# Transformer layer with linear attention on one core: loads cut in pieces on one queue, Wq transposed mid-stage, one numerator tile at a time, a tabulated unit order

## The chip, the cores and the metric

The kernel runs on one core of one Trainium2 chip. The metric is device time in microseconds (us) of one execution, inputs and outputs in HBM. A core has TensorE (PE, matmuls; its weight loads are PEld), VectorE (DVE), ScalarE (ACT), GpSimd (POOL) and SyncE (SP), which here only issues DMAs. Each engine runs its own instruction list strictly in order; semaphores tie the lists together.

## The reference

One pre-norm layer on x of 2048 rows by 640, all in bf16, with 32 heads of 20 columns:

```
n = layernorm(x);  q, k, v = n @ wqkv             # 640 -> 3 x 640
phi(a) = [softmax(a @ w_phi), softmax(-(a @ w_phi))]   # per head, 20 -> 40 features
o = phi(q) (phi(k)^T v) / (phi(q) . sum_s phi(k) + 1e-6)
h = x + o @ wo
h2 = h + ((layernorm(h) @ w_gate) * (layernorm(h) @ w_up)) @ w_down   # 640 -> 1536 -> 640
```

## The kernel before, in words

The 2048 rows are 16 tiles t of 128; the 640 columns are 5 chunks of 128. Everything is a graph of named units, built in `build_graph`; each unit is a few instructions of one engine. The names that matter:

- **WT, WTe, F1, Fe1** (lines 228 to 261): Wk arrives by rows, PE transposes it (WT), ACT or DVE copies it out (WTe), PE multiplies it with a block-diagonal w_phi (the fold F1), and the copy Fe1 gives the weight that yields k @ w_phi in one step. **wqt, F0, Fe0**: the same for Wq, whose transposes come from six DMA transposes straight from HBM (line 181). All five F0 need all six wqt.
- **x** loads (line 158); **L1s, L1a, L1l, L1e** layernorm statistics on DVE and ACT; **xn** (line 301, DVE) scales a tile to bf16; **xt** transposes it: on PE for the tiles in `TPE` (line 309, copy-out xte on ACT), for the others by a DMA transpose from SP (line 317).
- **K, V** (line 326): projections of a tile, ten matmuls of 320 columns each; **Kx** two exponentials (ACT), **Ks** sums (DVE, line 352), **Kr** reciprocals (DVE), **Kn** the multiply (GpSimd, line 357), **Ve** the copy-out of V (line 343), and **KV** (PE, line 366) accumulates phi(k)^T v over all tiles in three PSUM banks. This is the K/V stage.
- **Q** (line 385): a chunk of q features for 512 rows, then two exponentials Qx (ACT).
- **N** (line 414): numerator and denominator of a tile, two units (s = 1, 0), each with two PSUM banks; DVE combines them by **sr, rho, A, B, dd, rd**; **o** (line 446, GpSimd) divides; **oT** (SP, line 451) transposes; **O** (line 457) is the output projection; **h, L2s, L2a, L2v, L2r, hc, hT** residual, second statistics, centring and a DMA transpose (line 481).
- **U** (line 496): gate and up products in five row blocks (256, 512, 512, 512, 256), **g** copy-out, **u** product (DVE), **D** (line 514) the down projection, **y** (line 526) the scaled residual, **w** the store.

Who runs first is set by `schedule`: an event loop with assumed costs. Each unit has a key; whenever an engine of the loop is free, the ready unit with the lowest key that also finds its buffer slots (`NSLOTS`: PSUM has 8 banks) is appended to that engine's list. The lists are then emitted, with waits, and are what the chip executes in order. A DMA without inputs is ready at once, so its key only places it among other ready DMAs of that queue; SP issues it as soon as it comes up. In the version before, ACT's queue holds the loads of w_phi, of tiles 4 to 15 and of Wo; SP's holds the others.

PE's list before, up to the fourth tile: WT0 WT1 F1_0 F1_1 xt0 WT2 WT3 F1_2 F1_3 WT4 F1_4 F0_0 F0_1 K0 V0 F0_2 F0_3 F0_4 xt1 K1 V1 KV0 K4 V4 K2 V2 KV1 K3 V3 Q0_0. SP's list: x0 wk0 wk2 wk4 wv x1 x2 wqt0 to wqt5 wg wu, then xt4 xt5 xt2 and the other row transposes. All of Q0 stands ahead of KV15 in PE's list.

Of the kernel before, what the change touches and what calls it, by code (L numbers as in the profile page):

```python
# [124 lines left out]
def build_graph():  # L125
# [10 lines left out]


# [101 lines left out]
    FOLD = [(g, 20 * 6 * g, min(20 * 6 * g + 120, 640)) for g in range(6)]
    def fold(kind, i, key, eng):  # L240
# [16 lines left out]
        def fe(e):  # L257
            o = T["Wp"][:, kind, i, :].rearrange("p (b n) -> p b n", b=2)
            if eng == "dve":
                return e.tensor_copy(out=o, in_=pp(b, 0, 320))  # L260
            return e.activation(out=o, in_=pp(b, 0, 320), func=AF.Copy)
        G.op(eng, "Fe%d_%d" % (kind, i), fe, dve_c(640, True) if eng == "dve" else act_c(640), LD, [b], [wp_b[kind][i]], key)
# [35 lines left out]
    for t in range(NT):  # L298
# [5 lines left out]
        if t in TPE:  # L304
            b = Buf("pxt%d" % t, "psum")
            def xt(e, t=t, b=b, xb=xb):
# [6 lines left out]
            G.op("act", "xte%d" % t, lambda e, t=t, b=b: e.activation(  # L313
                out=T["xnT"][:, :, P * t:P * (t + 1)], in_=pb(b).bitcast(BF16)[:, 0:D].rearrange("p (c n) -> p c n", c=NC),
                func=AF.Copy), act_c(640), LA, [b], [xT_b[t]], 10 * t - 20)
# [87 lines left out]
    for t in range(NT):  # L403
        kk = 200 + 12 * t
        q = [i for i, (o0, n) in enumerate(QB) if o0 <= P * t < o0 + n][0]
        nb = {}
# [457 lines left out]
```

## Time and profile before

| what | value |
|---|---|
| median of 3 runs | 313.77 us (310.62 to 314.88) |
| the profiled execution | 312.41 us, span 310.5 us, mean granted clock 0.978 |
| PE busy | 277.5 us, 89% of the span |
| PE weight loads | 182.9 us, 59% |
| DVE busy | 177.6 us, 57% |
| ACT, POOL busy | 107.5 us (35%), 66.6 us (21%) |
| moved by DMA | 22.48 MB |

The page of the profile gives, in this order: busy time by engine; the span in 40 slices with the busy tenths of each engine, the granted clock of PE (in tenths of 2.4 GHz) and DMA activity; the DMA queues; the chain of work that ended last, followed backwards; the costliest groups of instructions with what they waited for; the DMA issues with their time to landing. A line such as L326 is a line of the kernel. SPq stands for SP's instruction queue (its DMA issues), which the page does not count as busy.

### The profile page before, as it was taken

The numbers are of one execution on the slowest core, as the hardware profiler recorded it, in microseconds if no ns is written. First come the engines' busy times: TensorE is split into PE (matmuls) and PEld (weight loads), VectorE is DVE, ScalarE is ACT, GpSimd is POOL, SyncE is SP. The second block draws the span as 40 slices with busy tenths as digits, with TensorE's granted clock in tenths as the row PEclk, the third lists the DMA queues.
The fourth block names the chain that finished last, engine by engine and source line by source line (L and its number), as shares of the span: only waits on it lengthen the run. The fifth ranks groups of instructions, "written<-read, shape, count | busy, mean of one in ns | idle before, by whom it ended". The sixth has DMA issues, their size and how long they took to land.

```text
span 310.5 us, 4962 instructions
## 1 busy us (share of the span) xinstructions
PE 277.5 (89%) x2041; PEld 182.9 (59%) x2058; DVE 177.6 (57%) x357; ACT 107.5 (35%) x189; POOL 66.6 (21%) x71
## 2 busy tenths in 40 slices
PE   3418699999999869979999999799999999999996
PEld 3315567767755538845565477545456754467874
DVE  3743999956547697393645367758454743332332
ACT  3407376555668434345412200223230113210220
POOL 6000267576741323012010011030101100000000
PEclk9857999999999999999999999999999999999999
DMA  8999534500000626122571103242111121001101
GB/s 247 343 222 405 142 65 86 86 1 2 2 0 0 67 52 77 22 44 42 169 149 42 21 5 85 64 62 41 25 21 43 47 61 23 0 0 48 39 2 43
DMA packets 45166, 22.48 MB, mean 72 GB/s; under 512 B 36183, under 2 KB 43863, under 8 KB 45143
## 3 DMA queue, kind: packets, MB, share of 16 engines
q1 hardware_dynamic: 42160, 19.34, 27.3%
q10 hardware_dynamic: 2983, 2.81, 2.9%
q8 instruction: 16, 0.26, 0.4%
q14 instruction: 7, 0.06, 0.1%
HBM read 11.01 MB, written 2.62 MB: 44 GB/s over the span
## 4 chain that ended last, share of the span: by engine, by line
PE 77%; DVE 8%; SPq 6%; DMA 4%; ACT 1%; issue 1%; POOL 1%; DVEq 0%
PE ps L496 33%; PE ps L514 17%; PE ps L326 12%; PE ps L457 6%; PE ps L385 5%; SPq L181 5%; PE ps L366 3%; DVE xn L301 2%; PE ps L414 2%; DVE x_all L461 2%; DMA scratch<-scratch 1%; DMA xnT<-xn 1%; SPq L158 1%; DMA scratch<-in_A_wqkv_dram 1%; DVE st L468 1%
## 5 line engine op out<-in xcount | busy, mean ns | idle before, releaser
L496 PE MATMUL ps<-xnT,Wgu 128*128 128x512 bf16 (+1 forms) x589 | 104.8, 336 | 2.8 <-DVE rs L473 1.9
L496 PEld LDWEIGHTS ps<-xnT,Wgu 128*128 128x128 bf16 x600 | 58.4, 98 | 46.7 <-DVE ev L504 3.4
L504 DVE TENSOR_TENSOR ev<-ps,scratch 128x512 bf16<-128x512 f32 (+1 forms) x60 | 35.0, 584 | 49.4 <-PE ps L496 48.4
L501 ACT ACTIVATE scratch<-ps 128x512 bf16<-128x512 f32 (+1 forms) x60 | 30.7, 511 | 90.7 <-PE ps L496 90.7
L514 PE MATMUL ps<-Wp,ev 128*128 128x320 bf16 x384 | 53.5, 299 | 0.5 <-DVE ev L504 0.5
L326 PE MATMUL ps<-Wp,xnT 128*128 128x320 bf16 x320 | 48.3, 307 | 2.8 <-DMA xnT<-xn 1.8
L357 POOL TENSOR_TENSOR ev<-ev,SR 128x1280 bf16<-128x1280 bf16 x16 | 37.8, 2364 | 44.6 <-DVE SR L355 35.9
L514 PEld LDWEIGHTS ps<-Wp,ev 128*128 128x128 bf16 x384 | 37.3, 98 | 15.5 <-DVE ev L504 0.8
L326 PEld LDWEIGHTS ps<-Wp,xnT 128*128 128x128 bf16 x320 | 31.3, 100 | 15.6 <-DMA xnT<-xn 2.0
L352 DVE TENSOR_REDUCE SR<-ev 128x64 f32<-128x1280 bf16 x16 | 23.7, 1484 | 19.8 <-ACT ev L349 19.7
L446 POOL TENSOR_TENSOR scratch<-scratch,sm 128x640 bf16<-128x640 f32 x16 | 20.2, 1270 | 65.7 <-DVE sm L443 61.6
L526 DVE SCALAR_TENSOR_TENSOR Wp<-ps,rs,x_all 128x640 bf16<-128x640 f32 (+1 forms) x17 | 14.4, 845 | 31.5 <-PE ps L514 31.5
L476 ACT ACTIVATE xn<-x_all,mv 128x640 bf16<-128x640 bf16 x16 | 13.2, 827 | 50.8 <-DVE mv L470 50.8
L349 ACT ACTIVATE ev<-ps 128x640 bf16<-128x640 f32 x32 | 20.8, 700 | 15.2 <-PE ps L326 15.2
L385 PE MATMUL ps<-xnT,Wp 128*128 128x512 bf16 x94 | 22.6, 379 | 3.9 <-DVE sm L429 2.0
L457 PE MATMUL ps<-Wo,scratch 128*128 128x320 bf16 x160 | 23.9, 299 | 1.5 <-DMA scratch<-scratch 0.9
L394 ACT ACTIVATE eqT<-ps 128x512 bf16<-128x512 f32 x40 | 21.6, 594 | 8.8 <-PE ps L385 8.8
L457 PEld LDWEIGHTS ps<-Wo,scratch 128*128 128x128 bf16 x160 | 15.4, 98 | 8.7 <-DMA scratch<-scratch 1.4
L471 POOL TENSOR_SCALAR ln<-mv 128x1 f32<-128x1 f32 x16 | 3.3, 208 | 77.4 <-DVE mv L470 77.4
L461 DVE TENSOR_TENSOR x_all<-ps,x_all 128x640 bf16<-128x640 f32 x16 | 13.1, 818 | 11.2 <-PE ps L457 11.2
L385 PEld LDWEIGHTS ps<-xnT,Wp 128*128 128x128 bf16 x100 | 9.4, 98 | 13.0 <-DVE scratch L432 3.7
L251 PE MATMUL ps<-Phi,scratch 120*128 120x120 bf16 (+3 forms) x70 | 5.0, 238 | 11.6 <-DMA scratch<-in_A_wqkv_dram 9.9
(49 smaller groups left out, 202.1 us busy)
## 6 DMA issues: line engine op xcount, KB each, us to landing
out_dram<-Wp SPq DMA_DIRECT2D x15, 160.0 KB, 1.8
Wgu<-in_B_w_gate_dram SPq DMA_DIRECT2D x1, 1920.0 KB, 9.2
Wgu<-in_B_w_up_dram SPq DMA_DIRECT2D x1, 1920.0 KB, 13.3
Wp<-in_B_w_down_dram SPq DMA_DIRECT2D x1, 1920.0 KB, 8.1
x_all<-in_A_x_dram ACTq DMA_DIRECT2D x1, 1280.0 KB, 13.2
Wp<-in_A_wqkv_dram SPq DMA_DIRECT2D x1, 800.0 KB, 10.1
Wo<-in_A_wo_dram ACTq DMA_DIRECT2D x1, 800.0 KB, 15.6
scratch<-in_A_wqkv_dram SPq DMA_DIRECT2D x2, 320.0 KB, 4.1
```

What stands on the lines that cost most here:

```text
L326: ins = e.matmul(pb(b, hb)[:, 0:320], lhsT=T["xnT"][:, c, P * t:P * (t + 1)], rhs=T["Wp"][:, kind, c, 320 * hb:320 * (hb + 1)], start=(c = ...
L349: G.op("act", "Kx%d_%d" % (t, s), lambda e, s=s, b=b, ek=ek: e.activation(out=T["ek"][:, ek.slots[0], s, :].rearrange("p (b n) -> p b n", ...
L352: G.op("dve", "Ks%d" % t, lambda e, ek=ek, sr=sr: e.tensor_reduce(out=T["SR"][:, sr.slots[0], 0, :], in_=T["ek"][:, ek.slots[0], :, :].rea ...
L357: G.op("pool", "Kn%d" % t, lambda e, ek=ek, sr=sr: e.tensor_tensor(out=T["ek"][:, ek.slots[0], :, :].rearrange("p s (h f) -> p (s h) f", f ...
L385: ins = e.matmul(pb(b)[:, 0:n], lhsT=T["Wp"][:, 0, i, P * c:P * (c + 1)], rhs=T["xnT"][:, i, o0:o0 + n], start=(i == 0), stop=(i == NC - 1))
L394: G.op("act", "Qx%d_%d_%d" % (q, c, s), lambda e, s=s, c=c, o0=o0, n=n, b=b: e.activation(out=T["eqT"][:, s, c, o0:o0 + n], in_=pb(b)[:, 0 ...
L446: G.op("pool", "o%d" % t, lambda e, sm=sm, B=B, o=o: e.tensor_tensor(out=T["o"][:, o.slots[0], :].rearrange("p (h d) -> p h d", d=DH), in0 ...
L457: ins = e.matmul(pb(b, hb)[:, 0:320], lhsT=T["oT"][:, oT.slots[0], c, :], rhs=T["Wo"][:, c, 320 * hb:320 * (hb + 1)], start=(c == 0), stop ...
L496: ins = e.matmul(pb(b)[:, 0:n], lhsT=T["Wgu"][:, gu, c, P * ft:P * (ft + 1)], rhs=T["xnT"][:, c, o0:o0 + n], start=(c == 0), stop=(c == NC ...
L501: G.op("act", "g%d_%d" % (bi, ft), lambda e, pg=pg, gt=gt, n=n: e.activation(out=T["gt"][:, gt.slots[0], 0:n], in_=pb(pg)[:, 0:n], func=AF ...
L504: o_ = G.op("dve", "u%d_%d" % (bi, ft), lambda e, pu=pu, gt=gt, hh=hh, ft=ft, n=n: e.tensor_tensor(out=T["hh"][:, hh.slots[0], ft, 0:n], i ...
L514: ins = e.matmul(pb(b, hb)[:, 0:320], lhsT=T["hh"][:, hh.slots[0], ft, P * tt:P * (tt + 1)], rhs=T["Wd"][:, ft, c0 + 320 * hb:c0 + 320 * ( ...
```

## The change

- The loads are cut (Wv in two, x in pairs of tiles, Wo in two, Wg and Wu in five each, Wd in four), all issued from SP. The loads from tile 8 on, the six wqt and the pieces of Wo, Wg and Wu get a `before` edge: they may be issued only after a given row transpose has been issued.
- The folds F0 and the six wqt move to the middle of the K/V stage.
- A pool `nt` with one slot: N with s = 1 of a tile takes it, dd of that tile frees it.
- Tile 2 is transposed on PE as well. A table `TUNED` replaces every key, and for copies out of PSUM and for o it may name the other engine (a 1 behind the second colon).
- The loop's assumed DMA costs change.

The core of the diff (of the table, its first lines):

```diff
-TPE = (0, 1)
+TPE = (0, 1, 2)
...
-          "sm": 4}
+          "sm": 4, "nt": 1}
+TUNED = {}
+for _t in """
+x0:1.18 wk0:2.14 wk2:2.62 wk4:4.06 x1:0.7 wv0:3.1 wv3:4.54 x2:3.58 x4:5.02 x6:1.66 phr:0.7 ph5:1.18 x8:15.21 x10:19.073 x12:24.913 x14:19.553
+wqt0:21.253 wqt1:22.473 wqt2:36.843 wqt3:35.623 wqt4:34.403 wqt5:39.283 wo0:43.163 wo2:42.203 wg0:41.723 wu0:42.683 wg1:49.725 wu1:54.085 wg2:48.025
...
+    _f = _t.split(":")
+    TUNED[_f[0]] = (float(_f[1]), int(_f[2]) if len(_f) > 2 else 0)
...
-        o.eng, o.name, o.emit, o.occ, o.lat, o.dma = eng, name, emit, occ, lat, dma
-        o.key = key + PRIO.get(name, 0.0)
+        o.alts = [(eng, occ, lat)] + list(alts)
+        k, a = TUNED.get(name, (key, 0))
+        o.eng, o.occ, o.lat = o.alts[a]
+        o.name, o.emit, o.dma = name, emit, dma
+        o.key = k
+        o.before = list(before)
...
+    def evac(name, f, n, reads, writes, key, dve=False):
+        a = [("act", act_c(n), LA), ("dve", dve_c(n, True), LD)]
+        if dve:
+            a.reverse()
+        return G.op(a[0][0], name, f, a[0][1], a[0][2], reads, writes, key, alts=a[1:])
...
-    xload("act", 4, 8, -60)
-    xload("act", 8, 16, -59)
-    dma("act", "wo", lambda: T["Wo"][:, :, :], lambda: T["A_wo"].rearrange("(c p) n -> p c n", p=P), 819, [wo_b], key=-58)
+    PACE = {t: [] for t in range(NT)}
...
+    for j in range(4):
+        PACE[3 + j].append(xload("sp", 8 + 2 * j, 10 + 2 * j, 10 * (3 + j) - 19))
     for g in range(6):
...
+        PACE[7 + g // 2].append(wqt(g, 10 * (7 + g // 2) - 19))
+    PACE[10] += [wrows("wo", lambda: T["Wo"], "A_wo", wo_b[0:2], 0, 2, 328, 81), wrows("wo", lambda: T["Wo"], "A_wo", wo_b[2:5], 2, 5, 492, 81)]
+    for c in range(NC):
+        PACE[11 + c] += [wrows("wg", lambda: T["Wgu"][:, 0], "B_wg", [wg_b[c]], c, c + 1, 393, 91 + 10 * c),
+                         wrows("wu", lambda: T["Wgu"][:, 1], "B_wu", [wu_b[c]], c, c + 1, 393, 91 + 10 * c)]
...
+            for o_ in PACE[t]:
+                o_.before.append(G.by["xt%d" % t])
...
+        nt = Buf("nt%d" % t, "nt")
...
-                 [eq_b[q, c, s] for c in range(NC)] + kvm_b + [kv1_b], [b], kk)
+                 [eq_b[q, c, s] for c in range(NC)] + kvm_b + [kv1_b], [b] + ([nt] if s else []), kk)
...
-            op0=ALU.mult, op1=ALU.add), dve_c(32, True), LD, [nb[0], B], [sm], kk)
+            op0=ALU.mult, op1=ALU.add), dve_c(32, True), LD, [nb[0], B], [sm, nt], kk)
...
             if o.dma > 0:
-                bw = max(bw, now + occ + 1.0) + o.dma / 390.0
-                o.end = bw + 0.4
+                bw = max(bw, now + 1.5) + o.dma / 340.0
+                o.end = bw + 0.28
             elif o.dma < 0:
-                o.end = now + o.lat
+                bw = max(bw, now + 1.85) + 0.5
+                o.end = bw + 0.28
```

The table read as an order (units sorted by key; that is how the lists come out as far as units are ready in that order):

```
SP:  x1 x0 x6 wk0 wk2 wv0 x2 wk4 wv3 x4 xt3 x8 xt4 xt6 x10 x14 xt7 wqt0 wqt1 xt5 x12 xt9 xt8 wqt4 wqt3 wqt2 xt10 wqt5 xt11
     wg0 wo2 wu0 wo0 xt13 wu2 wg2 xt12 wg1 xt15 xt14 wu3 wg3 wg4 wu1 wu4 oT1 oT0 oT2 hT1 hT0 oT3 hT2 wd0 wd2 wd1 wd3 oT5 ...
PE:  WT1 WT0 xt1 WT2 WT3 F1_1 F1_0 F1_3 xt0 WT4 F1_2 V1 F1_4 V0 K0 xt2 K1 K3 K2 K4 V6 K6 V7 V2 KV0 K7 KV1 K5 V3 KV2 V4 V5 V9 V8 K8 K9
     KV3 V10 KV4 F0_1 KV5 F0_0 K11 KV6 K10 V11 KV7 K13 KV8 V13 K12 K14 KV9 V14 K15 V12 KV10 F0_3 KV11 F0_2 KV12 F0_4 KV13 V15 KV14
     Q0_4 KV15 Q0_0 Q0_1 Q0_3 Q0_2 Q3_4 N1_1 Q1_2 N1_0 N0_0 Q1_3 Q1_4 N3_0 N0_1 Q3_2 Q2_3 N2_0 Q1_1 N2_1 Q2_1 Q2_0 O1 Q2_4 N3_1 ...
DVE, tiles 8 to 15 of xn:  ... Ks4 xn9 xn8 xn11 Ks5 xn10 Kr3 ... Fe0_0 xn13 Ks9 xn12 Ks11 xn15 Kr9 xn14 Ve11 ...
```

On DVE instead of ACT: Ve0, Ve1, Ve11, Ve15, Fe0_0, Fe0_2, Fe0_4; instead of GpSimd: o7, o10, o11, o13. On ACT instead of DVE: WTe1, Fe1_0, Fe1_2, Fe1_4.

## Rows read from the trace of the kernel before

**Rows 1.** The page's slices of the span: PE, busy tenths.
```profile
PE   3418699999999869979999999799999999999996
```

**Rows 2.** Busy time by stretch: window, length, PE, PEld, DVE, ACT, POOL, PEclk, DMA share, GB/s.
```profile
0.00:4.55 4.55, 0.00 (x0) 0.00 (x0) 1.10 (x3) 1.55 (x2) 2.49 (x13) 1.00 0.62 158
4.55:12.62 8.07, 6.36 (x70) 5.53 (x70) 5.87 (x14) 4.33 (x8) 2.78 (x11) 1.00 1.06 369
12.62:22.49 9.87, 0.00 (x0) 0.03 (x1) 4.81 (x14) 0.00 (x0) 0.00 (x0) 0.55 1.06 249
22.49:37.07 14.58, 10.69 (x92) 7.54 (x93) 8.00 (x18) 8.50 (x18) 2.36 (x1) 0.83 0.81 289
37.07:62.00 24.93, 24.76 (x220) 18.55 (x222) 23.73 (x39) 15.10 (x27) 15.10 (x7) 1.00 0.46 80
62.00:91.85 29.85, 29.30 (x266) 21.47 (x266) 15.35 (x16) 18.37 (x30) 20.32 (x9) 1.00 0.01 2
91.85:310.45 218.60, 206.41 (x1397) 129.80 (x1409) 118.78 (x256) 59.65 (x107) 23.53 (x32) 1.00 0.23 46
```

**Rows 3.** Waits of PE up to 92 us: waited in total, times, longest.
```profile
PE ps L251 <- DMA scratch<-in_A_wqkv_dram: 9.9, 1, 9.9
```

**Rows 4.** Chain of waits, 4 to 40 us: start, length, what.
```profile
4.36 4.27 SPq L181
...
19.26 3.10 DMA scratch<-in_A_wqkv_dram
...
23.72 4.57 PE ps L326 x20
```

**Rows 5.** Chain of waits, later in the stage.
```profile
74.62 2.72 PE ps L326 x20
...
89.01 2.16 PE ps L385 x10
91.17 0.68 PE ps L366 x12
```

**Rows 6.** Timeline, weight transposes (L228) and folds (L251) on PE: start, length, instructions.
```profile
7.85 1.48 PE L228 MATMUL ps<-ident,scratch 128*128 128x128 bf16 x12
...
28.11 1.06 PE L251 MATMUL ps<-Phi,scratch 120*128 120x120 bf16 x21
```

**Rows 7.** Busy time of two stretches of the K/V stage, columns as in rows 2.
```profile
3.08:91.85 88.77, 71.11 (x646) 53.11 (x649) 58.86 (x101) 46.57 (x82) 41.68 (x27) 0.92 0.50 137
...
30.00:62.00 32.00, 28.78 (x257) 21.46 (x259) 30.16 (x55) 19.03 (x35) 17.46 (x8) 1.00 0.50 104
```

**Rows 8.** Groups by line on DVE (B, xn, copy out of PSUM): busy us, mean ns of one, idle before.
```profile
L435 DVE TENSOR_TENSOR scratch<-ps,scratch 128x672 f32<-128x672 f32 x16 | 13.5, 843 | 0.2
...
L301 DVE TENSOR_SCALAR xn<-x_all,mv,rs 128x640 bf16<-128x640 bf16 x16 | 10.3, 666 | 1.4 <-ACT rs L284 0.7 <-DMA xnT<-xn 0.6
...
L260 DVE CAST Wp<-ps 128x640 bf16<-128x640 f32 x3 | 2.4, 802 | 0.1
```

**Rows 9.** Timeline at 31 us: a GpSimd multiply and an xn.
```profile
30.98 2.36 POOL L357 TENSOR_TENSOR ev<-ev,SR 128x1280 bf16<-128x1280 bf16 x1 [23.37 <-DVE SR L355]
...
31.55 1.97 DVE L301 TENSOR_SCALAR xn<-x_all,mv,rs 128x640 bf16<-128x640 bf16 x1
```

**Rows 10.** Single lines: duration ns min/median/max, first and last start.
```profile
L181 SPq DMA_TRANSPOSE scratch<-in_A_wqkv_dram x6: 1272/2363/4411, 4.4 to 19.3; - x6
...
L317 SPq DMA_TRANSPOSE xnT<-xn x14: 1199/1276/1641, 33.5 to 60.0; - x14
...
L301 DVE TENSOR_SCALAR xn<-x_all,mv,rs x16: 340/443/2481, 6.5 to 58.7; 128x640 bf16<-128x640 bf16 x16
```

**Rows 11.** Timeline of SP at 150 us, right behind the load of Wd (1920 KB).
```profile
150.48 4.71 SPq L481 DMA_TRANSPOSE xnT<-xn  x2
```

**Rows 12.** Busy time of two stretches behind the K/V stage, columns as in rows 2.
```profile
100.00:120.00 20.00, 15.71 (x126) 10.29 (x126) 16.85 (x45) 8.75 (x16) 7.21 (x9) 1.00 0.41 59
...
300.00:310.45 10.45, 7.18 (x53) 4.81 (x50) 2.41 (x4) 0.36 (x1) 0.00 (x0) 1.00 0.10 32
```

More of the change, by code (lines that the diff above doesn't have):

```diff
@@ new lines @@
+xn7:16.873 xt7:20.033 xn8:31.783 xt8:33.183 xn9:31.363 xt9:31.963 xn10:34.023 xt10:38.063 xn11:32.203 xt11:40.503 xn12:47.545 xt12:48.505 xn13:45.725
+xt13:46.325 xn14:50.335 xt14:51.425 xn15:49.365 xt15:50.205 V0:12.077 Ve0:14.53:1 K0:13.435 Kx0_0:15.063 Kx0_1:16.334 Ks0:17.293 Kr0:22.513 Kn0:23.243
+KV0:26.328 V1:10.416 Ve1:15.281:1 K1:15.461 Kx1_0:17.09 Kx1_1:17.9 Ks1:20.963 Kr1:24.463 Kn1:25.602 KV1:28.362 V2:24.97 Ve2:26.598 K2:18.178
+Kx2_0:19.911 Kx2_1:20.721 Ks2:23.063 Kr2:27.263 Kn2:27.993 KV2:31.755 V3:30.397 Ve3:32.077 K3:16.82 Kx3_0:18.5 Kx3_1:19.311 Ks3:25.863 Kr3:34.443
@@ new lines @@
+Kn3:35.173 KV3:40.581 V4:32.431 Ve4:34.059 K4:19.536 Kx4_0:21.322 Kx4_1:22.132 Ks4:29.963 Kr4:37.243 Kn4:39.891 KV4:42.615 V5:33.789 Ve5:35.418
+K5:29.038 Kx5_0:30.667 Kx5_1:31.477 Ks5:32.623 Kr5:34.993 Kn5:37.532 KV5:43.593 V6:20.895 Ve6:22.732 K6:22.253 Kx6_0:23.881 Kx6_1:24.692 Ks6:37.793
+Kr6:39.493 Kn6:42.25 KV6:46.032 V7:23.611 Ve7:25.292 K7:27.004 Kx7_0:28.632 Kx7_1:29.443 Ks7:40.043 Kr7:42.293 Kn7:44.609 KV7:49.424 V8:36.506
+Ve8:38.134 K8:37.864 Kx8_0:39.493 Kx8_1:40.303 Ks8:42.843 Kr8:44.423 Kn8:46.968 KV8:51.459 V9:35.148 Ve9:36.776 K9:39.223 Kx9_0:41.527 Kx9_1:42.337
@@ new lines @@
+Ks9:46.145 Kr9:49.785 Kn9:50.515 KV9:56.21 V10:41.257 Ve10:42.938 K10:46.708 Kx10_0:48.336 Kx10_1:49.146 Ks10:52.056 Kr10:54.856 Kn10:55.586
+KV10:60.961 V11:48.066 Ve11:50.755:1 K11:44.673 Kx11_0:46.302 Kx11_1:47.112 Ks11:47.965 Kr11:51.506 Kn11:52.874 KV11:61.939 V12:59.602 Ve12:61.283
+K12:53.493 Kx12_0:55.121 Kx12_1:55.932 Ks12:56.742 Kr12:59.553 Kn12:60.304 KV12:62.916 V13:52.135 Ve13:53.763 K13:50.1 Kx13_0:51.729 Kx13_1:52.539
+Ks13:53.456 Kr13:55.406 Kn13:57.945 KV13:63.894 V14:56.886 Ve14:58.514 K14:54.851 Kx14_0:56.532 Kx14_1:57.342 Ks14:58.153 Kr14:60.103 Kn14:62.663
@@ L59 @@
     __slots__ = ("i", "eng", "name", "emit", "occ", "lat", "deps", "acq", "bufs", "key", "dma", "ndep", "outs",
-                 "pos", "start", "end", "alldeps")
+                 "pos", "start", "end", "alldeps", "alts", "before", "nouts")
 class Graph:
@@ L256, in fold, with fe @@
         G.op("pe", "F%d_%d" % (kind, i), f, mm_c(120, 120, 80, 40, 120, 120, 40), LT, rd + [phi_b, phi5_b], [b], key)
[L257 to L262, printed above, removed]
+        def fe(e, eng):
+            return copy(e, eng, T["Wp"][:, kind, i, :].rearrange("p (b n) -> p b n", b=2), pp(b, 0, 320))
+        evac("Fe%d_%d" % (kind, i), fe, 640, [b], [wp_b[kind][i]], key, eng == "dve")
     for i in range(NC):
         fold(1, i, -88 + i, "act" if i % 2 else "dve")
-    for i in range(NC):
-        fold(0, i, 62 + i, "act")
-    grp = {}
     for t in range(NT):
@@ L312, in build_graph @@
             G.op("pe", "xt%d" % t, xt, mm_c(*[P] * 5), LT, [xb, id_b], [b], 10 * t - 20)
[L313 to L315 removed]
+            evac("xte%d" % t, lambda e, eng, t=t, b=b: copy(
+                e, eng, T["xnT"][:, :, P * t:P * (t + 1)], pb(b).bitcast(BF16)[:, 0:D].rearrange("p (c n) -> p c n", c=NC)),
+                 640, [b], [xT_b[t]], 10 * t - 20)
         else:
@@ L376, in build_graph @@
             dve_c(504, True), LD, [KVB[k], glx_b] + gl_b, [kvm_b[k]], 150)
+    for i in range(NC):
+        fold(0, i, 62 + i, "act")
     lastproj = []
@@ L397, in build_graph @@
     lastproj += [G.by["K%d" % t] for t in range(NT)] + [G.by["V%d" % t] for t in range(NT)]
-    dma("sp", "wd", lambda: T["Wd"], lambda: T["B_wd"].rearrange("(f p) n -> p f n", p=P), 1966, [wd_b], key=310, after=lastproj)
+    for k in range(4):
+        dma("sp", "wd%d" % k, lambda k=k: T["Wd"][:, 3 * k:3 * k + 3, :],
+            lambda k=k: T["B_wd"][3 * P * k:3 * P * (k + 1), :].rearrange("(f p) n -> p f n", p=P), 492, [wd_b[k]], key=310,
+            after=lastproj)
     h_b, hT_b, rs2_b, mv2_b = x_b, [], [], []
@@ L557, in schedule @@
         o.outs = []
+        o.nouts = []
     for o in ops:
-        o.ndep = len(o.deps)
+        o.ndep = len(o.deps) + len(o.before)
         for d in o.deps:
             d.outs.append(o)
+        for d in o.before:
+            d.nouts.append(o)
         o.start = None
@@ L600, in schedule @@
             _, _, kind, o = heapq.heappop(ev)
+            if kind == 0 and o is not None:
+                for d in o.nouts:
+                    d.ndep -= 1
+                    if d.ndep == 0:
+                        heapq.heappush(ready[d.eng], (d.key, d.i, d))
             if kind == 1:
```

151 lines of the change are left out of this document (111 added, 40 removed).

## The prediction

> **What bounds the kernel now.** I read the page's slices first [rows 1]: TensorE (PE) is nearly full from a seventh of the span on, and broken before. Cutting the span at the waits [rows 2] gives PE idle per stretch: 4.55 us before the first transpose, 1.71 in the chain of weight folds, 9.87 with nothing at all, 3.89 on the restart, 0.72 in the rest of the K/V stage (to 91.85), and 12.19 in the remaining 218.60: 32.9 of 310.45 us. So PE's work sets the time and the idle 32.9 is all there is to win, plus what a lowered clock cost.
>
> The list of waits names the 9.87 [rows 3]: the fold of Wq waits for DMA transposes of Wq. The chain of waits shows why [rows 4]: those six transposes have no inputs, so they sit on SP's queue right behind the first loads, at 4.36 us, and the first holds SP for 4.27 us; the last lands at 22.36. The folds of Wq stand in PE's order ahead of the first K, so everything queues behind them. The granted clock averages 0.55 over that gap [rows 2], so most of it is at the lower level (1.2 GHz), and the first K and V projections (20 matmuls) take 4.57 us where a later pair takes 2.72 [rows 4, 5]: 1.85 lost.
>
> Behind 91.85 us the idle sits in a few clusters [rows 12]: 4.29 us in 100 to 120 and 3.27 at the end (drain). In the first of these DVE is busy 16.85 of 20 us: numerators, residual and second layernorm of two tiles come bunched while PE has no other unit ready.
>
> **K/V stage, part by part.** To compare, take its end as the last KV accumulation: 91.17 plus 0.68 = 91.85 [rows 5]. Five Q units stand ahead of it in the old order, one (Q0_4) in the new; a Q unit is 1.08 (ten matmuls 2.16, five each). The same work would have ended at 91.85 - 4 x 1.08 = 87.5.
>
> *What PE needs.* Two weight transposes take 1.48 [rows 6], so five 3.7; ten folds at a third of 1.06 each are 3.5; three row transposes of five matmuls are 1.9 at the same rate; 32 projections of 1.36 are 43.5; 16 KV at 0.68 are 10.9; one Q 1.08. Sum 64.6. The start: two x tiles, x6-7 and the first Wk piece now come in front on one queue, 960 KB against 480; at 369 GB/s [rows 2] that is at most 1.3 later, at least 0.4 (the other queue's loads no longer share the rate); I take 0.9, so 5.4. If PE never waits, the stage ends at 70.0.
>
> *What DVE needs.* It was busy 58.86 from 3.08 to 91.85 [rows 7]. The table moves seven PSUM copies to it (four V, three Wq folds; 0.80 each [rows 8]) and four away (about 3.0): 61.5. In its densest stretch before it reached 30.16 of 32, 94%. 61.5/0.94 = 65.4, so its last reciprocal ends at 68.5; GpSimd's multiply of 2.36 [rows 9], a KV of 0.68 and 0.2 of hops make 71.7.
>
> The limits lie 1.7 us apart and feed each other (projection, exponent, sum, multiply, KV), and the start still has PSUM copies between PE steps; I add 1.3 and put the end at 73.0. Gain: 87.5 - 73.0 = 14.5. Bounds: 70.0 (17.5) and, with 85% of DVE reached, 3.1 + 72.4 + 3.2 = 78.7 (9).
>
> *Wq moved.* Six transposes go behind row transposes 7, 8 and 10, the folds behind V10 and KV4. An undisturbed one occupies SP 1.27 and lands in 3.1 [rows 4, 10]. The last is issued right behind row transpose 10 and lands some 1.7 us after it; V10 and KV4, which need tile 10 or stand behind it, hide 2.0. That cover is thin: each us more comes out on PE, since all five folds need all six pieces, and KV5, K11 and what follows queue behind them.
>
> *Loads on SP.* Three issues leave ACT's queue (nothing there was late: its first wait is for DVE) and 20 more plain loads enter SP's, 30 instead of 10. A transpose ahead of which a load waits delays nothing but that load, none needed soon. The opposite order matters: seven pieces of Wo, Wg and Wu stand ahead of or between row transposes 13, 12, 15 and 14, and SP is one in-order queue: projections 12 to 15 wait for those four. Behind 1.9 MB a transpose held SP 2.36 (two: 4.71 [rows 11]) instead of 1.27. Bounds: 0, and 4 x 1.1 = 4.4 us; I take 1, near the low end, as at most 0.8 MB lies between two of them. It is inside the 1.3.
>
> Pieces of 160 to 800 KB, issued back to back, moved 369 GB/s at the start [rows 2], so the cutting itself is charged at nothing. The Trainium skill, "DMA: Bandwidth & Descriptors", section Bandwidth, speaks against it: loads should be batched to 1 MiB or more to reach three quarters of the peak. By that page's 341 GB/s for 1 MB, as an estimate of the best case, the first 2.9 MB would end some 0.7 us later and the sum would be that much higher.
>
> *DVE beside GpSimd.* A layernorm scale (xn) takes 0.34 to 2.48, median 0.44 [rows 10]; one of 1.97 starts 0.57 us after a GpSimd multiply and ends with it [rows 9]. In the new order xn13 and xn12 stand behind sums at a point where GpSimd has a run of multiplies without break: up to 1.9 each. Before, the same collisions cost 16 x (0.67 - 0.44) = 3.6 in all, already in the 58.86; I add nothing. The Trainium skill, "SBUF — State Buffer", section Who interferes with whom, calls the port pair that DVE and GpSimd share an exclusive lock, held for the whole instruction of whoever comes first. With the 1.97 the trace agrees; what that would do to a DVE without slack is rival 3.
>
> **Behind the K/V stage.** PE's work stays: 218.60 - 12.19, plus four Q units. One numerator tile in flight adds a wait: the first N of a tile waits for the previous tile's dd on DVE, and the whole of PE queues behind it. DVE needs some 2.2 us from the second N to dd (two of 0.84 [rows 8], small ones); in the new order three to five units (Q at 1.08, U0 at half of that) stand between, some 3 to 4.5 us. Covered by about 1 us each, and PSUM is left for U units that can run meanwhile. Four output multiplies move from GpSimd to DVE, each between 0.44 (an xn) and 2.36 (a GpSimd multiply of twice the size), nearest 0.84 [rows 8], which also takes two inputs in fp32: 3.4 on an engine that is 54% busy here [rows 2]: nothing on the path. Interleaving U0 and U1 with the numerators should break the clusters, but in-order queues with covers of 1 us do not hold everywhere. Of the 9.4 that are not the final drain I take back half, 4.7; bounds 0 and 9.4, and 5 lost.
>
> **Sum.** 14.5 + 4.7 = 19.2. The profiled execution is 312.41 (span 310.45 and 1.96 around it): 293.2. The median shown is 0.4% above it (313.77), so the forecast is **294.5 us**.
>
> **Rivals.**
> 1. *The clusters behind the stage only move* (their gain is 0 or slightly negative): 294.5 + 4.7 to + 8 = 299 to 302.5. For: covers of 1 us. Against: DVE has room on average. Chance 0.18.
> 2. *Everything fits*: the stage ends at 70.0 and the clusters go: 294.5 - 3.0 - 4.7 = 287. Chance 0.13.
> 3. *The port lock paces DVE*: the eight xn of tiles 8 to 15, held up to 1.9 each (2.36 - 0.44), add 15 to a DVE without slack: 309, no measurable change; with half of them, 302. For: 1.97 [rows 9]. Against: 3.6 in all before, with as many multiplies. Chance 0.07.
> 4. *SP's queue becomes the bound; slower.* Of the six old transposes two took 4.3 to 4.4 us of SP beside saturated loads [rows 4, 10]. Nineteen transposes now share SP with the loads of the stage. If each held it 4.3, 19 x 3.0 = 57 less some 10 of slack, 47 us more: 341.5. It decides where the mean hold passes some 3.0 us: (3.0 - 1.27) x 19 - 10 = 23, and 294.5 + 23 = 317.5. Against: 2.36 behind 1.9 MB, and 1.64 at most for row transposes beside the last of Wu [rows 10]; the loads are now spread. Chance 0.05.
> 5. *The order does not hold on the chip*: the table is only a list of priorities; if waits at the start (Wk's last piece arriving late, so that K0 and all behind it slip 6 us) shift one engine against the others: 300 to 305. Chance 0.07.
>
> **How the numbers follow.** The forecast itself (289 to 299) has 0.50. Range: 285, where rival 2 and a start without loss meet, to 306, where the stage's 9 and nothing behind it meet (312.4 - 9 + 1.4 = 305). 2% of 313.8 is 6.3 us, about what a measurement here can tell from no change: faster means under 307.5. Faster: 0.50 + 0.18 + 0.13 + 0.07 (rivals 1, 2, 5) and a little of rival 3: 0.89; same: 0.06, the rest of rival 3; slower: 0.05, rival 4.
>
> **What would show it.** No PE wait on a transpose of Wq and a granted clock that stays at full after the first fold; last KV near 73, with DVE over 90% busy until then; SP's row transposes 12 to 15 at about 1.3 to 2.4 us each; xn near 0.44 except a few; behind it no DVE-caused PE wait over 2 us. I am wrong if the last KV comes past 79, if PE waits for xnT there by several us, or if waits for DVE behind it add up to over 9.

## The result, and the profile after

The changed kernel takes 289.62 us (median of 4 runs, 287.41 to 290.11) against 313.72 beside it: ratio 0.9244, 95% interval 0.9168 to 0.9319. Its profiled execution took 287.41 us, span 285.7. The forecast was 294.5 (285 to 306).

The page's slices of PE and of its granted clock, after:

```profile
PE   0999999899999999999999999999999999999996
PEclk9999999999999999999999999999999999999999
```

The holes of [rows 1] are gone, and no lowered clock is recorded (what the column shows at the very start is taken up in the last section).

Windows of after, cut at its waits and at the end of the last KV (columns as in [rows 2]):

```profile
0.00:6.61 6.61, 0.00 (x1) 0.01 (x1) 2.66 (x8) 1.78 (x3) 4.36 (x21) 1.00 0.74 212
6.61:12.17 5.56, 5.36 (x69) 5.18 (x70) 4.15 (x13) 4.53 (x9) 1.33 (x3) 1.00 0.80 283
12.17:25.59 13.42, 13.14 (x103) 9.20 (x103) 13.08 (x29) 10.79 (x21) 1.34 (x1) 1.00 0.57 135
25.59:54.28 28.69, 26.89 (x261) 20.74 (x261) 26.07 (x45) 15.93 (x27) 20.35 (x10) 1.00 0.68 142
54.28:72.81 18.53, 18.53 (x203) 14.68 (x204) 12.57 (x15) 8.66 (x14) 15.65 (x7) 1.00 0.53 182
72.81:285.70 212.89, 209.90 (x1431) 132.36 (x1429) 121.45 (x260) 63.82 (x115) 18.52 (x28) 1.00 0.21 47
3.08:72.81 69.73, 63.92 (x633) 49.81 (x634) 58.48 (x105) 40.40 (x71) 40.62 (x27) 1.00 0.65 171
```

PE is idle 8.89 us in the K/V stage (72.81 - 63.92), 6.61 of it before the first transpose, and 2.99 behind the stage, where it was 12.19 [rows 2]. Of DVE's 69.73 us, 58.48 are busy, 84%; in the stage's last 18.53 us PE is full and DVE is not.

All waits of PE in after (waited in total, times, longest):

```profile
PE ps L345 <- DMA scratch<-in_A_wqkv_dram: 6.6, 1, 6.6
PE ps L437 <- DMA xnT<-xn: 2.0, 3, 1.1
PE ps L569 <- DMA scratch<-scratch: 0.2, 1, 0.2
PE ps L437 <- ACT Wp L228: 0.2, 1, 0.2
```

None is for a transpose of Wq [rows 3] and none for DVE. From the chain of waits of after, three stretches (start, length, what):

```profile
2.18 4.38 DMA scratch<-in_A_wqkv_dram
...
48.92 5.31 DMA xnT<-xn
54.23 0.05 issue
54.28 1.53 PE ps L437 x10
...
72.13 0.68 PE ps L472 x12
```

Wk's first piece, fourth on SP's queue, lands 4.38 us after its issue; one row transpose among the pieces of Wg and Wu lands after 5.31 (PE waits 1.1 us for it, the longest such wait above); the last KV ends at 72.81. Single lines of after (ns min/median/max, first and last start): xn, the row transposes, Wq's transposes; then the last of DVE's reciprocals (start, length).

```profile
L410 DVE TENSOR_SCALAR xn<-x_all,mv,rs x16: 340/440/1249, 6.5 to 53.4; 128x640 bf16<-128x640 bf16 x16
```

```profile
L426 SPq DMA_TRANSPOSE xnT<-xn x13: 1199/1275/1520, 15.3 to 54.5; - x13
```

```profile
L288 SPq DMA_TRANSPOSE scratch<-in_A_wqkv_dram x6: 1271/1271/1290, 23.0 to 42.0; - x6
```

```profile
66.91 0.55 DVE L461 RECIPROCAL SR<-SR 128x64 f32<-128x64 f32 x1
```

Against [rows 10], Wq's six no longer hold SP for up to 4.41 us, and xn's longest is halved.

**Where the 24.75 us of span came from.** K/V stage: 87.5 (91.85 with four more Q units) to 72.81, 14.7. Behind it: 218.60 to 212.89 with those four units, 4.3, added: 10.0, of which PE's idle time gives 9.2 (12.19 - 2.99). The profiled execution of after is the lowest of its four, 2.2 us under the median; that of before lies 1.3 under its own.

### The profile page after: what moved, and what is told of

It is laid out like the page before. It is cut to its first block, busy times and chain, and to the rows that moved or that the text cites. A ratio compares the mean times of both kernels' runs of the same rounds, so it can differ in the third digit from the quotient of the medians.

```text
span 285.7 us, 4989 instructions
## 1 busy us (share of the span) xinstructions
PE 273.8 (96%) x2063; PEld 182.2 (64%) x2063; DVE 180.0 (63%) x365; ACT 105.5 (37%) x186; POOL 61.6 (22%) x67
## 4 chain that ended last, share of the span: by engine, by line
PE 87%; DMA 7%; DVE 2%; ACT 2%; SPq 1%; issue 0%; DVEq 0%
PE ps L608 34%; PE ps L626 18%; PE ps L437 11%; PE ps L569 8%; PE ps L493 8%; PE ps L526 4%; PE ps L472 3%; DMA xnT<-xn 3%; DMA scratch<-scratch 2%; DMA scratch<-in_A_wqkv_dram 2%; SPq L259 1%; PE ps L366 1%; DVE SR L458 1%; PE ps L345 1%; ACT scratch L228 0%; ACT ev L455 0%
## 5 line engine op out<-in xcount | busy, mean ns | idle before, releaser
L608 PE MATMUL ps<-xnT,Wgu 128*128 128x512 bf16 (+1 forms) x600 | 108.0, 336 | 0.0
L616 DVE TENSOR_TENSOR ev<-ps,scratch 128x512 bf16<-128x512 f32 (+1 forms) x60 | 33.4, 575 | 34.8 <-PE ps L608 18.6
L437 PE MATMUL ps<-Wp,xnT 128*128 128x320 bf16 x320 | 46.0, 299 | 2.3 <-DMA xnT<-xn 2.0
L626 PEld LDWEIGHTS ps<-Wp,ev 128*128 128x128 bf16 x384 | 37.5, 98 | 14.7
L437 PEld LDWEIGHTS ps<-Wp,xnT 128*128 128x128 bf16 x320 | 30.4, 98 | 14.7 <-DMA xnT<-xn 3.3
L558 POOL TENSOR_TENSOR scratch<-scratch,sm 128x640 bf16<-128x640 f32 x12 | 15.3, 1271 | 59.3 <-DVE sm L555 41.0
L502 ACT ACTIVATE eqT<-ps 128x512 bf16<-128x512 f32 x40 | 21.6, 594 | 11.2 <-PE ps L493 11.1
L493 PE MATMUL ps<-xnT,Wp 128*128 128x512 bf16 x100 | 23.5, 379 | 0.0
L526 PEld LDWEIGHTS ps<-KVm,eqT 128*128 128x128 bf16 x192 | 12.9, 98 | 4.4 <-issue 0.2
L526 PE MATMUL ps<-KVm,eqT 128*128 128x154 bf16 (+1 forms) x192 | 15.5, 221 | 0.0
```

The source lines that it names most:

```text
L437: ins = e.matmul(pb(b, hb)[:, 0:320], lhsT=T["xnT"][:, c, P * t:P * (t + 1)], rhs=T["Wp"][:, kind, c, 320 * hb:320 * (hb + 1)], start=(c = ...
L493: ins = e.matmul(pb(b)[:, 0:n], lhsT=T["Wp"][:, 0, i, P * c:P * (c + 1)], rhs=T["xnT"][:, i, o0:o0 + n], start=(i == 0), stop=(i == NC - 1))
L502: G.op("act", "Qx%d_%d_%d" % (q, c, s), lambda e, s=s, c=c, o0=o0, n=n, b=b: e.activation(out=T["eqT"][:, s, c, o0:o0 + n], in_=pb(b)[:, 0 ...
L526: ins = e.matmul(pb(b, y)[:, 22 * h0:22 * (h0 + j1 - j0)], lhsT=T["eqT"][:, s, c, P * t:P * (t + 1)], rhs=T["KVm"][:, OFF[s, c] + j0:OFF[s ...
L608: ins = e.matmul(pb(b)[:, 0:n], lhsT=T["Wgu"][:, gu, c, P * ft:P * (ft + 1)], rhs=T["xnT"][:, c, o0:o0 + n], start=(c == 0), stop=(c == NC ...
L616: o_ = G.op("dve", "u%d_%d" % (bi, ft), lambda e, pu=pu, gt=gt, hh=hh, ft=ft, n=n: e.tensor_tensor(out=T["hh"][:, hh.slots[0], ft, 0:n], i ...
```

## The experiments

The theory was the prediction's: Wq's place on SP costs the K/V stage its 12 us, the table's order the rest. Its rivals: pacing of the big loads, and the one-tile limit. Where an edit says "lists held", PE, DVE, ACT and GpSimd keep their lists unit by unit, so that only the named thing moves. In the runs on the kernel before, and where the table is emptied or shortened, the planner makes new lists.

### Wq moved alone, in the kernel before (b_wq)

```diff
+            for g in range(6):
+                if t == 7 + g // 2:
+                    G.by["wqt%d" % g].before.append(G.by["xt%d" % t])
```

> The kernel before with one part of the change alone: the six transposes of Wq are issued behind row transposes 7, 8 and 9, and the folds of Wq follow from that; loads, keys and numerators are as before. My theory: this part alone brings the idle 9.87 us in front of the first K and V and the 1.85 us of low clock, less what DVE, which now starts its sums about 10 us earlier, cannot follow: 301 to 304 us against 313.7. Rival: the row transposes and DVE set the pace of the K/V stage anyway and only the place of the wait changes: 309 to 314. Seen in the trace: last KV (with all five Q0 ahead of it) at 80 to 83 by the theory, over 88 by the rival.

314.39 us, ratio 1.0033 (0.9998 to 1.0068): **no gain, the theory fails**; the last KV ends at 94.06 us, where the theory had 80 to 83 and the rival over 88. Its longest wait of PE, the chain that leads to it, and DVE's line before it:

```profile
PE ps L330 <- DMA xnT<-xn: 8.8, 1, 8.8
```

```profile
2.37 16.57 DMA x_all<-in_A_x_dram
...
20.22 10.00 DMA xnT<-xn
```

```profile
18.96 0.49 DVE L274 BATCH_NORM_STATS2 st<-x_all 128x6 f32<-128x320 bf16 x1 [2.46 <-DMA x_all<-in_A_x_dram]
```

Without Wq's transposes in front of them on SP, the 3.9 MB of Wg and Wu are issued at 5.0 and 5.9 us. Tiles 8 to 15, on ACT's queue since 2.37, now land 16.57 us after issue; DVE holds the statistics of tile 8 ahead of xn of tiles 4 and 5 in its list, so these and their row transposes start late, and the first transpose lands after 10.00 us instead of some 2.7, about when the last of Wu does (5.9 plus 23.7). The kernel before had the first part of this stall too, under PE's wait for Wq: DVE waited for tile 8 until 15.62 us there, with xn of tiles 1 and 4 behind it in its list.

```profile
15.62 0.49 DVE L273 BATCH_NORM_STATS2 st<-x_all 128x6 f32<-128x320 bf16 x1 [1.54 <-DMA x_all<-in_A_x_dram]
```

Wq's transposes had cost 9.87 us and had, by standing there, kept Wg and Wu back. The lists are not those of before, though: with Wq late the planner puts K4, V4, K5 and V5 ahead of K1. The move with the old lists held was not run, so what part of the new stall comes from the order stays open.

### The same, and Wg and Wu paced too (b_wq_pace)

```diff
+            if t in (11, 15):
+                G.by["wg" if t == 11 else "wu"].before.append(G.by["xt%d" % t])
```

> The kernel before with the transposes of Wq mid-stage as in b_wq, and Wg and Wu (still whole) issued only behind row transposes 11 and 15. In b_wq the two big loads moved up to 5 us with the Wq transposes gone from in front of them, and x of tiles 4 to 7 landed 16.6 us after its issue. Theory now: the Wq transposes had also held Wg and Wu back; with both out of the way the stage gets its 10 us: 301 to 304 us, last KV (all of Q0 ahead of it) at 80 to 83. Rival: x of tiles 8 to 15, Wo and the order of units keep the start late: over 309.

The load that took 16.6 us in b_wq is that of tiles 8 to 15; that of tiles 4 to 7 took 9.1.

303.32 us, ratio 0.9675 (0.9649 to 0.9701), and the last KV ends at 81.87, both as expected. PE, DVE, ACT and GpSimd have the lists of b_wq, so the 11.1 us between the two runs are the pacing's. The two loads are still whole, still 1.9 MB each. DMA issues without this edit (b_wq) and with it (KB each, median us from issue to landing):

```profile
Wgu<-in_B_w_gate_dram SPq DMA_DIRECT2D x1, 1920.0 KB, 18.8
...
x_all<-in_A_x_dram ACTq DMA_DIRECT2D x1, 1280.0 KB, 16.6
x_all<-in_A_x_dram ACTq DMA_DIRECT2D x1, 640.0 KB, 9.1
```

```profile
Wgu<-in_B_w_gate_dram SPq DMA_DIRECT2D x1, 1920.0 KB, 9.3
...
x_all<-in_A_x_dram ACTq DMA_DIRECT2D x1, 1280.0 KB, 13.4
x_all<-in_A_x_dram ACTq DMA_DIRECT2D x1, 640.0 KB, 6.7
```

and PE's wait for row transposes, 8.8 before:

```profile
PE ps L332 <- DMA xnT<-xn: 2.2, 2, 1.6
```

So the two edits together give the 10 us: there were two stalls, one under the other's cover, and each edit takes away one. Pacing without the move was not run. The Trainium skill, "DMA: Bandwidth & Descriptors", section Issuing engines are not separate DMA queues, says that transfers of all issuing engines interleave on the same 16 DMA engines; these rows agree: loads on ACT's queue land 2.4 and 3.2 us later for what SP has issued.

### The changed kernel with the old loads (a_loads)

Lists held (ACT's with its three loads put back); whole loads on two queues, Wg and Wu unpaced, Wq still mid-stage.

```diff
+TUNED.update({"x0": (0.7, 0), "wk0": (0.8, 0), "wk2": (0.9, 0), "wk4": (1.0, 0), "wv0": (1.1, 0), "x1": (1.2, 0), "x2": (1.3, 0),
...
-    xload("sp", 4, 6, -92)
-    xload("sp", 6, 8, -91)
+    xload("act", 4, 8, -60)
+    xload("act", 8, 16, -59)
...
-        PACE[3 + j].append(xload("sp", 8 + 2 * j, 10 + 2 * j, 10 * (3 + j) - 19))
```

> The changed kernel with the loads of before: whole, x of tiles 4 to 15 and Wo on ACT's queue, Wg and Wu whole on SP right behind the first ones, none paced; the transposes of Wq stay mid-stage and the order of units on PE, DVE, ACT and GpSimd is the same. My theory: 9 MB are then in flight until about 24 us, row transposes issued from 15 us on hold SP for 2.4 to 4.4 us and land behind them, so the third K starts 5 to 9 us late: 294 to 299. Rival: row transposes pass beside the loads and the earlier arrival of x makes up for it: 287 to 291.

296.44 us, ratio 0.9464 (0.9398 to 0.9530), 6.8 us over after. PE's longest wait, the chain to it, SP's issues at its start, and the load of tiles 4 to 7 (KB, us to landing):

```profile
PE ps L460 <- DVE xn L452: 9.5, 1, 9.5
```

```profile
3.20 10.61 DMA x_all<-in_A_x_dram
```

```profile
3.20 1.16 SPq L305 DMA_DIRECT2D x_all<-in_A_x_dram  x2
```

```profile
x_all<-in_A_x_dram ACTq DMA_DIRECT2D x1, 640.0 KB, 6.5
```

The time came as expected, the mechanism did not. The load that lands after 10.61 us is that of tile 1: with the old loads it stands sixth on SP's queue, behind Wk and the whole of Wv, while DVE's held list begins with tile 1's statistics, so DVE starts at 13.84 us. Tiles 4 to 7 land 6.5 us after their issue, and no row transpose holds SP for more than 1.32 us. So this run shows what the place of one load of 160 KB costs an order that was made for another; it prices neither the cutting nor the pacing.

### Wq's transposes at the front again, in the changed kernel (a_wqearly)

Same unit order on the compute engines.

```diff
+for _g in range(6):
+    TUNED["wqt%d" % _g] = (5.5 + 0.1 * _g, 0)
...
-        PACE[7 + g // 2].append(wqt(g, 10 * (7 + g // 2) - 19))
+        wqt(g, 0)
```

> The changed kernel with the six transposes of Wq put back right behind the first loads on SP; the order of units on PE, DVE, ACT and GpSimd is the same as in the changed kernel, so the folds stay in the middle of the stage. My theory: SP is held while the first loads run, 2.4 to 4.4 us each for those that fall into them and 1.27 for the rest, some 14 us from 6 us on, so the first row transpose (at 15.3 in the changed kernel) goes out near 20: 3 to 6 us slower, 293 to 296. Rival: SP had nothing to do there (it idles from 6 to 15 us) and all the cost before came from the folds' place in PE's order: within 1 us, 289 to 291.

287.24 us, ratio 0.9172 (0.9111 to 0.9234): **no loss**; the rival was right. SP's timeline:

```profile
6.00 10.00 SPq L290 DMA_TRANSPOSE scratch<-in_A_wqkv_dram  x6
16.22 1.63 SPq L428 DMA_TRANSPOSE xnT<-xn  x1
```

The six now take 10.00 us, in a stretch in which SP had nothing to issue in after, and the first row transpose follows at 16.22 instead of 15.3. Two things differ from the kernel before: no fold at the head of PE's list waits for them, which the next run tests, and nothing of 1.9 MB stands behind them, which is not separated here.

### Wq's folds at the front too (a_foldearly)

On top of the kernel above: the five F0 ahead of K0 in PE's list, their copies all on ACT ahead of K0's exponentials (three were on DVE).

```diff
+    TUNED["F0_%d" % _g], TUNED["Fe0_%d" % _g] = (13.0 + 0.1 * _g, 0), (13.0 + 0.1 * _g, 0)
```

> The kernel a_wqearly (changed kernel, Wq transposed behind the first loads, which cost nothing) with the five folds of Wq put ahead of the first K in PE's order, as in the kernel before, their copies on ACT ahead of K0's exponentials; other orders as they were. Theory: what hurts is the folds' place in PE's in-order list, not the transposes: the last of them lands near 19, so K0 starts near 21 instead of 14: 5 to 8 us slower than a_wqearly, 292 to 296. Rival: with paced loads the folds' wait is caught up later because DVE bounds the stage: within 2 us, 287 to 290.

291.27 us, ratio 0.9302 (0.9250 to 0.9354): 4.0 us more, between the two ranges expected. The wait is back, small:

```profile
PE ps L414 <- DMA scratch<-in_A_wqkv_dram: 2.3, 1, 2.3
```

So of Wq's two parts it is the folds' place on PE that costs, because PE's list behind them cannot run on. Part of the 4 us is the clock: in the profiled execution (293.85) the granted clock behind this wait is 0.50 from 19.71 to 22.53 us. In the two whose mean granted clock is 1.00 (290.10 and 290.37) the place still costs some 3 us.

### Two numerator tiles in flight (a_nt2), and one in the kernel before (b_nt)

The first with the same lists; the second is the limit alone, with the old keys.

```diff
-          "sm": 4, "nt": 1}
+          "sm": 4, "nt": 2}
```

```diff
-          "sm": 4}
+          "sm": 4, "nt": 1}
...
-                 [eq_b[q, c, s] for c in range(NC)] + kvm_b + [kv1_b], [b], kk)
+                 [eq_b[q, c, s] for c in range(NC)] + kvm_b + [kv1_b], [b] + ([nt] if s else []), kk)
```

> The changed kernel with two numerator tiles allowed instead of one; the order of units on every engine comes out the same, so only the waits differ. My theory: the wait never binds, because three to five units stand between: no change, 289 to 291. Rival A: the wait binds at some of the sixteen numerators: 1 to 3 us faster. Rival B: without it PSUM slots are taken in another way and PE stalls: 2 us slower or more.

> The kernel before with one numerator tile at a time and nothing else of the change. Theory: behind the K/V stage the idle of PE comes from the bunched order of units, which this alters only in part: 1 to 4 us faster, 309 to 312. Rival A: two numerator tiles holding all eight PSUM banks were the cause: 5 to 9 us faster, 304 to 308. Rival B: the added wait costs: 315 or more.

a_nt2: 289.54 us, ratio 0.9220 (0.9171 to 0.9268), as after. b_nt: 344.19 us, 1.0968 (1.0923 to 1.1013), **31 us slower than before**, on the side of rival B (315 or more). Windows of b_nt:

```profile
140.00:160.00 20.00, 13.06 (x80) 7.94 (x80) 6.62 (x14) 0.90 (x2) 1.48 (x2) 0.83 0.51 132
160.00:200.00 40.00, 30.07 (x164) 15.54 (x167) 23.38 (x52) 8.41 (x13) 5.91 (x8) 0.87 0.23 33
```

PE's list there reads "O1 N3_1 N4_0 N5_0 N6_0 O2 U0_0_0": the limit is taken by N with s = 1 only, so the planner sends N with s = 0 of three later tiles ahead, and each keeps two of eight PSUM banks until its own tile gets the slot. In the list up to three tiles stand so at once, from N6_0 to N11_0. That the rest has to go through the banks left is read from the list, not isolated; PE is idle 16.9 of these 60 us, and its granted clock sinks to 0.83 and 0.87. A limit in a list planner is no limit unless everything that the waiting unit needs is behind it. The table's list has two tiles so at most, and behind N3_1 never more than one.

### The table taken away: all (a_notable), all with the limit off (a_notable_nt4), and kept up to the last KV (a_tabkv)

The first empties the table; the second also has four slots; the third has four slots and drops the table's entries over 68 us, so formula keys rule behind the K/V stage.

```diff
+    if float(_f[1]) > 68:
+        continue
```

> The changed kernel with an empty table: the formula keys and default engines, all else of the change kept (pieces on SP, pacing, Wq mid-stage, one numerator tile, tile 2 on PE). Theory: pacing and Wq give the K/V stage's gain, the order gives what is gained behind it (about 9): 297 to 300. Rival A: the table gives next to nothing: 289 to 292. Rival B: the table gives nearly all: over 305.

> The kernel after, with the table empty and four numerator slots instead of one, so that the limit practically never binds; all else as in the kernel after without its table (338.2 us). Theory: it is the limit of one slot, met by the planner's formula keys, that costs the 338: with the limit off the run looks like the kernel before with Wq's transposes and the big loads paced (303.3 us), so 298 to 306 us, and no PE waits of over 2 us around 120 to 200 us. Rival: the formula keys are bad for the cut loads on one queue whatever the limit: above 320 us. Between: both.

> The kernel after, with the table's entries kept only where they are below 68 us (the loads and the K/V stage), formula keys for everything behind, and four numerator slots so that the limit plays no part. It tells what the table's order behind the K/V stage is worth. Theory: most of the 10 us gained behind the stage come from the table's interleaving of numerators, Q, U and O units; then the K/V stage still ends near 72.8 us, and the waits of the old order return: 296 to 301 us. Rival: the stage behind became faster by itself (no Q units left in a hurry, Wd and buffers there in time): 288 to 292 us.

338.17 us (ratio 1.0775, 1.0723 to 1.0828), 306.49 (0.9787, 0.9728 to 0.9845) and 295.69 (0.9441, 0.9383 to 0.9498). None lies in the range of its theory, the last two by under 1 us, and the first is over 305, where rival B gave the table nearly all. But the limit met by formula keys is what made it slow: 31.7 us go with it. The windows behind the last KV, of b_wq_pace, a_notable_nt4 and a_tabkv (each starts 0.16 to 0.17 us before that KV's end, while PE is full):

```profile
81.70:301.10 219.40, 207.98 (x1399) 130.94 (x1411) 118.82 (x256) 59.94 (x108) 23.63 (x32) 0.99 0.20 46
```

```profile
86.25:304.40 218.15, 207.62 (x1414) 129.99 (x1411) 118.81 (x256) 59.91 (x108) 23.53 (x32) 1.00 0.23 46
```

```profile
72.32:291.70 219.38, 211.21 (x1434) 132.07 (x1431) 118.50 (x256) 64.11 (x116) 23.60 (x32) 1.00 0.21 46
```

PE's idle time there is 11.4, 10.5 and 8.2 us, against 12.2 before and 3.0 after. So of the 9.2 gained, the table's order behind the stage gives 5.2 (6.1 in the medians, 295.69 to the 289.54 of a_nt2), and 2.3 to 4 come with the four Q units that the table's K/V part leaves for later; that these fill PE's gaps is argued, not isolated. Up to the last KV the table moves its end from 86.4 (five Q units ahead of it) to 72.5 (one), and the time by 10.8. Set against the 87.5 of before, with one Q unit for all, the change without its table ends the stage at 82.1, 5.4 earlier, and the table gives 9.6 more; b_wq_pace, with the old keys and loads, gives 10.0. So what moving and pacing are worth depends on the order of units that they meet.

### An earlier start (a_start, a_start2)

On top of a_wqearly, PE's order held: Wk's first piece first on SP, identity and Phi first on GpSimd; then also x1 ahead of it, and tile 1 normalized first.

```diff
+TUNED.update({"wk0": (0.5, 0), "x1": (0.6, 0), "x0": (0.7, 0), "wk2": (0.8, 0), "wk4": (0.9, 0), "x6": (1.0, 0), "wv0": (1.1, 0), "x2": (1.2, 0)})
```

```diff
+TUNED.update({"x1": (0.5, 0), "wk0": (0.6, 0), "x0": (0.7, 0), "wk2": (0.8, 0), "wk4": (0.9, 0), "wv0": (1.0, 0), "wv3": (1.1, 0), "x2": (1.2, 0), "x6": (1.3, 0)})
```

> The kernel after with Wq's transposes right behind the first loads (287.2 us before this), now also with Wk's first piece as the first load of SP, the identity and Phi first on GpSimd, and xn1 ahead of the statistics of tile 6 on DVE; PE's order unchanged. Theory: PE's first transpose starts near 5.0 us instead of 7.0, and as PE waits for little after that, most of the 2 us stay: 285 to 286.5 us. Rival: the K/V stage is bound by DVE, which starts no earlier: its last KV accumulation stays near 72.5 us and the time at 287 to 288 us.

> As the kernel with Wk first (287.5 us), where PE started at 4.29 us but waited 2.42 for xn1, which stood behind the statistics of tile 0: now x1 is the first load and Wk's first piece the second, and on DVE tile 1 is normalized ahead of tile 0's statistics, tile 6's statistics come behind xn0. PE's order unchanged. Theory: PE has no wait of over 1 us after its start near 4.7 us, the first V projection comes near 11 us instead of 12.3, the last KV near 71.5 us, and the time is 285.5 to 286.7 us. Rival: the K/V stage is bound by DVE's sums behind 30 us, so the last KV stays at 72.5 us and the time at 287 to 288 us.

287.46 us (ratio 0.9182, 0.9146 to 0.9218) and 288.59 (0.9227, 0.9183 to 0.9272): nothing gained, by another cause than the rival's. The two longest waits of PE in a_start, and those of a_start2 with its timeline and clock:

```profile
PE ps L392 <- DMA scratch<-in_A_wqkv_dram: 4.3, 1, 4.3
PE ps L465 <- DVE xn L457: 2.4, 1, 2.4
```

```profile
PE ps L392 <- DMA scratch<-in_A_wqkv_dram: 4.6, 1, 4.6
PE ps L484 <- ACT Wp L275: 2.7, 1, 2.7
```

```profile
16.92 2.72 PE L484 MATMUL ps<-Wp,xnT 128*128 128x320 bf16 x10 [2.74 <-ACT Wp L275]
```

```profile
18.00:22.00 4.00, 4.00 (x26) 2.68 (x23) 3.26 (x9) 2.49 (x6) 0.00 (x0) 0.69 0.51 125
```

PE's idle time only moves: what starts 2.3 us earlier waits for the next loads (x1 and x0 in the first, whose statistics stand ahead of xn1; in the second x6, for which DVE waits 1.91 us with the statistics of tiles 2 and 3 behind it, and ACT's last fold copy stands behind the logarithm of those). The three kernels with Wq early lie 0.4 to 0.8% under after's median, with intervals that overlap its own; none is shown to be better.

## Why the prediction was right in its number, step by step

- **End of the K/V stage**, predicted 73.0 (5.4, 64.6 and 3.0 on top), measured 72.81 (6.61, 63.92 busy and 2.28 idle). PE's need held. The start did not: it came 2.06 us later than before, where 1.3 had been the most. The loads were charged at 369 GB/s, and moved 212 up to there and 283 in the next stretch (rows of after above). The 369 had been read as the rate of pieces of 160 to 800 KB; in that stretch ACT's loads of 640 and 1280 KB were in flight too. The prediction's estimate from the Trainium skill, "DMA: Bandwidth & Descriptors", section Bandwidth, would have added some 0.7 by the end of 2.9 MB. The measured 1.2 at the start lies on its side, but a_start, with Wk first and pieces of the same sizes, starts at 4.29, so the place in the queue decides, not the size. The DVE limit of 71.7 did not bind: DVE had 58.48 us of work instead of 61.5 and was busy 84%, not 94%, its last reciprocal ended at 67.46 (68.5 foreseen), and at the end PE is the full one. That a late start met less work and less idle time is luck of about 1.2 us. Whether a lighter DVE would shorten the middle of the stage was not tried.
- **"Wq moved"** as the origin of the 9.87 idle and 1.85 of clock: wrong, the step that failed. Moved alone, in the lists that the planner then makes, it gives nothing (b_wq); with the big loads paced it gives 10 us (b_wq_pace); and in the finished kernel the transposes may stand at the front again (a_wqearly). The chain of waits [rows 4] names only the latest of two late things; behind Wq's transposes stood tiles 4 to 15 and their row transposes, late already in before (15.62 us) and later for the sake of 3.9 MB that nobody needed yet. The prediction had found nothing late on ACT's queue and had called the next late thing DVE and PE's own work. It held in number because the diff contains the pacing too, and an order that can use both: without the table the stage gains 5.4 (a_notable_nt4).
- **SP's holds**, 1 us for row transposes 12 to 15: they held SP 1.20 to 1.52 us, at the low end of the 1.3 to 2.4 foreseen; one landed after 5.31 us and cost PE 1.1, and all of PE's waits for row transposes sum to 2.0. Right in size; rival 4 (holds over 3.0) did not occur.
- **xn and GpSimd**, nothing added: longest 1.25 us instead of the possible 1.9; rival 3 fell. The collisions stay rare: median 440 ns, as before.
- **One numerator tile**, covered by about 1 us each: right for the table (a_nt2 is the same). The prediction took the limit for a wait only; that it also changes which units the planner sends ahead, and costs 31 us without a table, it had not seen.
- **Behind the stage**, 4.7 taken back of 9.4: measured 9.2 to 10.0, at the upper bound. Mis-sized: the table leaves PE no wait for DVE at all. With formula keys there (a_tabkv) 8.2 us stay idle, so 5.2 of the gain are shown to be the order's; rival 1 (the clusters only move) did not occur.

So 14.5 became 14.7 and 4.7 became 10.0; 5.5 us more than forecast by the spans, 4.9 by the medians.

## What to carry to other kernels

A wait that the chain names may cover a second one that ends at nearly the same time: before crediting its removal, ask what the freed queue will issue next and whose loads that slows. Large loads without inputs go as early as the queue allows; tie each to a point of the work after which its bandwidth is free, and check by moving them alone. Where a planner makes the lists, moving one unit moves others, and lists that are held can bring a stall of their own (a_loads): look which load the first unit of each list needs. A buffer limit in a list planner must cover every unit that holds something for the waiting one, or it fills the memory with halves.

## What the runs showed of the hardware

- A load on one queue is slowed by later ones on another: 1280 KB on ACT's queue landed 13.4 us after issue (b_wq_pace), and 16.6 with 3.9 MB issued on SP's some 3 us behind it (b_wq); the first row transpose beside these took 10.00 us to land, where the median is 2.7.
- Wq's DMA transposes held SP 1.27 us each among paced pieces (after), 1.67 on average right behind the first loads (a_wqearly), up to 4.41 beside the whole loads of Wv, x and Wo [rows 10].
- In a_start2 a gap of PE of 2.74 us was followed by a mean granted clock of 0.69 over four us, a mean of its two levels, and ten projection matmuls took 2.72 us instead of 1.52.
- The column of the granted clock does not show the level of a run's first matmuls. In a_start the five matmuls that transpose a tile take 0.71 us behind a gap of 2.42 us, and those of another tile 0.44 three us later:

```profile
8.17 0.71 PE L465 MATMUL ps<-ident,xn 128*128 128x128 bf16 x5 [2.42 <-DVE xn L457]
...
11.37 0.44 PE L465 MATMUL ps<-ident,xn 128*128 128x128 bf16 x5
```

  The column is 1.00 for both. The same five at 19.43 us in a_start2, at a granted clock of 0.50, take 0.74. So no gap this early shows whether it lowers the clock.
